# A batch pair's side work in an attention step: directly behind the transposes of exponents, in place of behind the values

## The chip, the cores and the metric

One core of a Trainium2 chip runs the kernel; the other seven are idle. The metric is the device time of one launch in microseconds (us). TensorE is called PE here, its weight loads PEld, VectorE DVE, ScalarE ACT, GpSimd POOL; SyncE (SP) only issues transfers.

## The reference

Attention with eight batches, eight heads, 576 positions and 64 channels feeds a mixture of experts. Four heads see a local window, four see every 32nd position:

```python
mask_local = (rel >= 0) & (rel < stride)                    # stride = 32
mask_strided = (rel >= 0) & (pos[None, :] % stride == pos[:, None] % stride)
scores = np.where(masks[None], scale * q @ k.transpose(0, 1, 3, 2), -1e9)
attn = np.exp(scores - scores.max(-1)); attn /= attn.sum(-1) + 1e-09
x = (attn @ v).transpose(0, 2, 1, 3).reshape(4608, 512)     # one row per token
logits = x @ w_gate + modality_bias[modality_id]            # 8 experts
e_idx = np.argmax(logits, axis=1)
for e in range(8):
    out[mask] = gate_w[mask, None] * (np.maximum(x[mask] @ w1[e], 0) @ w2[e])
```

Everything is float32. Each token goes to one expert only.

## The kernel before

**Units and steps.** The batches are taken in four pairs. A pair has eight units: local and strided ones in turn (classes `Local` and `Strided`), each for one local head of both batches or two strided heads of one batch. The main loop (L1185) runs over steps n. It is a pipeline: step n does the scores of unit n, the turn of unit n-2 and the values of unit n-3. `masks` writes the additive masks of unit n+1 into PSUM with a small bf16 product, one step ahead; `scores` adds the products of queries and keys onto them (L354 local, L449 strided), and DVE takes the maximum (L361), subtracts it (L364) and ACT exponentiates. `turn` transposes the exponents on PE (L224, tiles `t` or `ts`), and ACT or DVE copies them out. `values` multiplies them with the values (L391 and L397 local, tile `o`; L499 strided, tile `ot`).

**Order.** PE's order is that of the program (`manual_schedule`). On the other engines a scheduler sets it, save for instructions that are pinned. All products and transposes write into one pool of eight PSUM buffers (`pa`), one bank each, so an instruction that starts a tile waits until an earlier tile in its buffer has been read out.

**Pieces.** When a pair's units are done, its outputs still have to be brought into both layouts (rows of tokens, and columns for the router), routed and stored. This side work is cut into pieces, one for a step. `turn_rows` (L508) transposes one strided output block, four transposes in tile `xs`; `finish_pair` (L516) is a generator whose pieces `pop` takes one by one (L1123). With the last unit of a pair called 7, the pieces of a pair are: four transposes in step 8 and in step 9 (`xs`); eight in step 10 (`xl`, local outputs); ten in step 11 (`xl`, four buffers); the router's logits in step 12 (`lg`, L597 and L602); the transposes of the logits and four of `xs`, seven in all, in step 13; six in step 14 (`xs`, three buffers); and the ranks in step 15 (`rk`, L663 and L664). From step 13 on a row of small instructions on DVE (L623 to L680) computes each token's expert and its place. ACT copies the transposes out (L514 for `xs`, L524 for `xl`). The next pair's units run at the same time. The fourth pair has only the first two pieces inside the loop; the rest stands beside the first expert slot.

**Loads.** SP issues the loads of unit n+3 at the head of step n, the second part behind the scores of unit n. The values of unit n-1 are loaded in two parts, the second behind the products of values of this step (`after_landing`, L1217).

**Experts.** After the loop the tokens go through slots of 384 rows that share an expert: L1022 up, L1037 down, with each float32 operand split into two parts (L1058, L1059), so three products for one.

The lines that the change touches are at the end of a step:

```python
        if n + 2 < nu:
            units[n + 2].prep()
        ready = len(stores) if n >= HOLD else 9
        if n - 1 in ends or n - 2 in ends:
            turn_rows(*ends[n - 1 if n - 1 in ends else n - 2], 0 if n - 1 in ends else 1, 0)
        pop(POPS if n == nu + 2 else 1)
```

Of the kernel before, what the change touches and what calls it, by code (L numbers as in the profile page):

```python
# [41 lines left out]
POPS, POPF = 5, 3  # L42
# [6 lines left out]
EARLY, BEGIN, HOLD = 3, 27, 26  # L49
# [142 lines left out]
def attention_moe(ctx: ExitStack, tc: tile.TileContext, a, out):  # L192
# [7 lines left out]
    def pa(name):  # L200
        return ps.tile([P, 512], F32, tag="a", name=name)
# [7 lines left out]
    def keep_busy(n, name):  # L209
        t = pa(name)  # L210
        for _ in range(n):
            nc.tensor.matmul(t, idle[:, 0:P], idle[:], start=True, stop=True)  # L212
# [10 lines left out]
    def turned_to(dst, src):  # L223
        return nc.tensor.transpose(dst, src, ident)  # L224
# [14 lines left out]
    def routing_setup():  # L239

        pin(nc.sync.dma_start(rt[:], a["rt"]))
        pin(nc.sync.dma_start(ld[0:1, :], a["nul"][:, 0:2]))
        pin(nc.sync.dma_start(xd[NT:NT + 1, :].bitcast(I32), a["nul"][:, 2:2 + DM]))
        modf = lp.tile([P, 36], F32, bufs=1, name="modf")
        pin(nc.gpsimd.tensor_copy(modf[:], modi))
        nmod = lp.tile([P, 36], F32, bufs=1, name="nmod")
        pin(nc.gpsimd.tensor_scalar(nmod[:], modf[:], -1.0, 1.0, ALU.mult, ALU.add))
        bias0 = lp.tile([P, 36, E], F32, bufs=1, name="bias0")

        def bc_e(t):  # L250
            return t.unsqueeze(2).to_broadcast([P, 36, E])

        def bc_t(t):
            return t.unsqueeze(1).to_broadcast([P, 36, E])

        pin(nc.gpsimd.tensor_tensor(bias[:], bc_e(modf), bc_t(mb[:, 1, :]), ALU.mult))
        pin(nc.gpsimd.tensor_tensor(bias0[:], bc_e(nmod), bc_t(mb[:, 0, :]), ALU.mult))
        pin(nc.gpsimd.tensor_tensor(bias[:], bias[:], bias0[:], ALU.add))
# [46 lines left out]
    class Local:  # L305
# [62 lines left out]
        def turn(self):  # L368
            n, ex = self.n, self.ex
            self.et = et = ets[0]  # L370
            t1 = pa(f"t1{n}").rearrange("p (g q) -> p g q", g=4)
            for k in range(4):
                turned_to(t1[:, k, :], ex[:, 2 * k:2 * k + 2, :])
            t2 = pa(f"t2{n}")[:, :P]
            self.point = turned_to(t2, ex[:, 9:11, :])
            for par in range(2):
                r = slice(64 * par, 64 * par + 64)
                nc.scalar.copy(et[r, 0:16, par, :], t1[r].rearrange("p k (u q) -> p (k u) q", u=4))
            for jj in range(2):
                r = slice(64 * jj, 64 * jj + 64)  # L380
                nc.scalar.copy(et[r, 16:18, jj, :], t2[r, 64 * jj:64 * jj + 64].rearrange("p (b q) -> p b q", b=2))
# [127 lines left out]
    def turn_rows(bp, xt, xcs, c, k0):  # L509
        kn = min(4, 9 - k0)  # L510
        t = pa(f"xs{bp}{c}{k0}").rearrange("p (g q) -> p g q", g=4)
        for k in range(kn):
            turned_to(t[:, k, :], xcs[2 + c][:, P * (k0 + k):P * (k0 + k + 1)])
        nc.scalar.copy(xt[:, k0:k0 + kn, 256 + P * c:256 + P * c + P], t[:, :kn, :])  # L514
# [64 lines left out]
    stores, tabulating = [], []  # L579
# [281 lines left out]
    def after_landing(ins, other):  # L861
        tc.add_manual_dep(ins.ins, other.ins.name, landed, reason="transfers kept apart")
# [216 lines left out]
    units, ends = [], {}  # L1079
# [10 lines left out]
    def after(bp, xt, xcs):  # L1090
        yield from finish_pair(bp, xt, xcs)
        if bp >= EARLY:
            yield
            yield from tabulate(bp)
# [10 lines left out]
    def pop(k):  # L1105
        for _ in range(k):
            early.clear()
            while extra:
                got = next(extra[0], extra)
                if got is not extra:  # L1110
                    early.extend([got] if got else ())
                    break
                extra.pop(0)
# [43 lines left out]
    def issue(count):  # L1157
        for _ in range(count):
            if queue and (queue[0][0] >= len(plan) or plan[queue[0][0]][1] in tables):
                queue.pop(0)[1]()  # L1160
# [10 lines left out]
    nu = len(units)  # L1171
# [12 lines left out]
    for n in range(nu + 3):  # L1184
        if n + 3 < nu:  # L1185
            units[n + 3].load(0)
        if n in FILL:
            keep_busy(FILL[n], f"warm{n}")
        if n < nu:
            units[n].scores()  # L1190
        waited = bool(early)
        if n + 3 < nu:
            after_landing(units[n + 3].load(1), units[n].scored)
        if waited:
            pop(1)
        if 2 <= n <= nu + 1:
            units[n - 2].turn()
        if 1 <= n <= nu:
            ins = units[n - 1].load_values(0)
            if n >= 2:  # L1200
                after_landing(ins, units[n - 2].point)
        if n + 1 < nu:
            units[n + 1].masks()
        if n == nu + 1:
            turn(0)
        if n >= 3:
            units[n - 3].values()
        if 1 <= n <= nu:
            ins = units[n - 1].load_values(1)
            if ins and n >= 3:  # L1210
                after_landing(ins, units[n - 3].valued)
        if n >= 3:
            if n - 3 in ends:
                extra.append(after(*ends[n - 3]))
        if n == SETUP:
            routing_setup()
        if n + 2 < nu:  # L1217
            units[n + 2].prep()
        ready = len(stores) if n >= HOLD else 9
        if n - 1 in ends or n - 2 in ends:  # L1220
            turn_rows(*ends[n - 1 if n - 1 in ends else n - 2], 0 if n - 1 in ends else 1, 0)
        pop(POPS if n == nu + 2 else 1)
        for _ in range(min(ready, STORED.get(n, SPREAD[(n - 2) % 8]))):
            if stores:
                stores.pop(0)()
        if n >= BEGIN:
            issue(2)
        if n in TABLES:
            for _ in tabulating[-1]:
                break  # L1230
# [83 lines left out]
```

## Time and profile before

| What | us |
|---|---|
| Runs of the kernel | 580.5, 583.21, 588.86 |
| Median of the three | 583.21 |
| Profiled execution | 581.83 |
| Span of that execution, first to last instruction | 580.0 |
| Attention with all its side work (span's start to the first expert product) | about 151 |
| Expert slots | about 422 |

The span and the launch around it make the execution's own time: 581.83 is 1.83 us more than the span, and 1.38 us less than the median of the runs. Times in the rows below count from the span's start. A busy engine is one that has an instruction in flight; products on PE overlap, so the start of one to the start of the next tells more than its duration.

### The profile page before, as it was taken

Reading aid. Unit: us, or ns where it says so; the run is one execution under the profiler, and the core shown is the slowest. Engines: PE = TensorE matmul, PEld = TensorE weight load, DVE = VectorE, ACT = ScalarE, POOL = GpSimd, SP = SyncE. Lnnn points to the kernel's source line nnn. Section 1 sums busy time; section 2 is a strip of 40 time slices with the busy share of each in tenths; the row PEclk is TensorE's granted clock in tenths of the full one; section 3 lists DMA queues with packets and bytes.
Section 4 is the critical chain, followed back from the end, with each engine's and each line's share of the span. In section 5 each row is a group of like instructions: output and inputs, shape, how many; then the busy total and the mean of one; then the engine's idle time right before and its main releaser. Section 6 shows DMA issues by size and latency. Waiting matters only on the chain.

```text
span 580.0 us, 13584 instructions
## 1 busy us (share of the span) xinstructions
PE 564.3 (97%) x5383; PEld 495.1 (85%) x5385; DVE 381.7 (66%) x909; ACT 325.0 (56%) x646; POOL 197.2 (34%) x198
## 2 busy tenths in 40 slices
PE   9999999998999999999999999999999999999995
PEld 5878888877788899989999998989898998998884
DVE  7886977967867874676674757666475666655410
ACT  5789898897744544554454544545363555545312
POOL 3011120125464315444344334554434445320102
PEclk9999999999999999999999999999999999999999
DMA  8988898978985308566543266142414156772102
GB/s 299 332 287 298 287 326 292 327 229 296 313 296 196 118 12 308 187 199 223 154 164 74 61 211 216 47 88 73 90 33 99 52 200 174 262 162 72 56 0 76
DMA packets 62699, 104.28 MB, mean 180 GB/s; under 512 B 36451, under 2 KB 36963, under 8 KB 58532
## 3 DMA queue, kind: packets, MB, share of 16 engines
q0 software_dynamic: 15456, 57.47, 28.6%
q1 hardware_dynamic: 45636, 43.29, 25.5%
q10 hardware_dynamic: 1536, 2.58, 1.4%
q8 instruction: 44, 0.72, 0.5%
q14 instruction: 27, 0.22, 0.1%
HBM read 94.09 MB, written 19.18 MB: 195 GB/s over the span
## 4 chain that ended last, share of the span: by engine, by line
PE 82%; issue 10%; ACT 3%; DVE 2%; POOL 1%; POOLq 0%; ACTq 0%
PE h L1022 31%; PE o L1037 30%; PE s L354 3%; PE ss L449 3%; PE o L391 2%; PE ot L499 2%; PE lg L597 2%; PE xl L224 2%; PE t L224 2%; PE xs L224 1%; PE warm L212 1%; PE ts L224 1%; POOL out L1044 1%; ACT xc L507 1%; PE en L695 1%
## 5 line engine op out<-in xcount | busy, mean ns | idle before, releaser
L1059 DVE TENSOR_TENSOR wl<-raw,wh 128x512 fp32r<-128x512 f32 x176 | 115.2, 692 | 66.8 <-ACT wh L1058 56.7
L1058 ACT CAST wh<-raw 128x512 fp32r<-128x512 f32 x176 | 100.5, 619 | 99.4 <-PE o L1037 81.5
L1022 PE MATMUL h<-xh,wl 128*128 128x384 f32 x352 | 118.7, 337 | 0.0
L1022 PE MATMUL h<-xl,wh 128*128 128x384 f32 x352 | 118.2, 336 | 0.0
L1022 PE MATMUL h<-xh,wh 128*128 128x384 f32 x352 | 117.4, 337 | 0.0
L1037 PE MATMUL o<-wl,hh 128*128 128x512 f32 x264 | 104.1, 394 | 0.0
L1037 PE MATMUL o<-wh,hl 128*128 128x512 f32 x264 | 104.0, 395 | 0.0
L1037 PE MATMUL o<-wh,hh 128*128 128x512 f32 x264 | 103.2, 391 | 0.0
L1025 ACT ACTIVATE hh<-h 128x384 fp32r<-128x384 f32 x88 | 43.2, 491 | 82.4 <-PE h L1022 71.0
L1027 DVE SCALAR_TENSOR_TENSOR hl<-h,hh 128x384 fp32r<-128x384 f32 x88 | 48.9, 555 | 56.5 <-ACT hh L1025 55.1
L921 POOL DMA_INDIRECT raw<-in_w,wi x44 | 51.8, 1177 | 61.3 <-ACT hh L1025 50.8
L1022 PEld LDWEIGHTS h<-xh,wh 128*128 128x128 f32 x352 | 66.2, 188 | 4.2 <-PE xs L224 0.4
L1022 PEld LDWEIGHTS h<-xl,wh 128*128 128x128 f32 x352 | 66.1, 188 | 2.9
L1022 PEld LDWEIGHTS h<-xh,wl 128*128 128x128 f32 x352 | 66.0, 188 | 0.4 <-DVE wl L1059 0.4
L889 POOL DMA_INDIRECT fx<-xd,le x33 | 37.2, 1129 | 76.8 <-ACT wh L1058 42.2
L1037 PEld LDWEIGHTS o<-wh,hl 128*128 128x128 f32 x264 | 49.5, 188 | 10.5
L1037 PEld LDWEIGHTS o<-wl,hh 128*128 128x128 f32 x264 | 49.5, 188 | 8.6
L1037 PEld LDWEIGHTS o<-wh,hh 128*128 128x128 f32 x264 | 49.6, 188 | 8.2
L906 POOL DMA_INDIRECT le<-ld,li x33 | 35.5, 1076 | 41.9 <-DVE li L828 17.6
L1044 POOL DMA_INDIRECT out<-y,le x33 | 34.6, 1049 | 41.3 <-ACT y L1043 37.0
L589 POOL DMA_DIRECT2D xd<-xt x18 | 10.0, 558 | 64.9 <-ACT xc L507 28.2
L983 DVE COPY work<-fx 128x1536 uint16<-128x1536 uint16 x16 | 27.2, 1743 | 0.0
(215 smaller groups left out, 872.6 us busy)
## 6 DMA issues: line engine op xcount, KB each, us to landing
vv<-in_vl SPq DMA_DIRECT2D x32, 292.5 KB
qks<-in_qks SPq DMA_DIRECT2D x32, 288.0 KB
qk<-in_qkl SPq DMA_DIRECT2D x16, 304.0 KB
qk<-in_qkl SPq DMA_DIRECT2D x16, 288.0 KB
xd<-xt POOLq DMA_DIRECT2D x18, 256.0 KB
vsp<-in_vs SPq DMA_DIRECT2D x16, 256.0 KB
xd<-xt SPq DMA_DIRECT2D x9, 256.0 KB
xd<-xt ACTq DMA_DIRECT2D x2, 1024.0 KB
```

Source lines behind the costliest of these rows:

```text
L224: return nc.tensor.transpose(dst, src, ident)
L889: ins = in_turn(nc.gpsimd.indirect_dma_start(xt[:, h, :], None, xd[0:xrows, :], IOA(ap=le[:, h, 0:1], axis=0), **bounds))
L906: in_turn(nc.gpsimd.indirect_dma_start(le[:, h, :], None, ld[0:1 + last, :], IOA(ap=li[:, s, h:h + 1], axis=0)))
L921: ins = nc.gpsimd.indirect_dma_start(raws[j].rearrange("p f c -> p (f c)"), None, a["w"], IOA(ap=wi[:, s, j:j + 1], axis=0), bounds_check= ...
L983: pin(nc.vector.tensor_copy(rows[:, :, w, :], halves(xt)[:, :, :, w]))
L1022: nc.tensor.matmul(hp, w[:, a1], x[:, c, 0:size], start=(k == 0), stop=(k == 11))
L1025: steps.append(nc.scalar.activation(hh[:, 0:size], hp, AF.Relu))
L1027: nc.vector.scalar_tensor_tensor(hl[:, 0:size], hp, 0.0, hh[:, 0:size].bitcast(F32), ALU.max, ALU.subtract)
L1037: nc.tensor.matmul(os[h], hx[:, m], w[:, 512:1024], start=(f == 0 and i == 0), stop=(f == 7 and i == 2))
L1044: outs.add(in_turn(nc.gpsimd.indirect_dma_start(out, IOA(ap=le[:, i, 0:1], axis=0), y[:], None, bounds_check=NT - 1, oob_is_err=False), True))
L1058: nc.scalar.copy(wh[:, c], raw[:, c])
L1059: nc.vector.tensor_tensor(wl[:, c], raw[:, c], wh[:, c].bitcast(F32), ALU.subtract)
```

## The change

The two statements on the pieces are moved up, from the end of a step to directly behind `turn`. A piece that is popped in the step in which its pair was only just handed over (n-3 in `ends`, step 10 in the counting above) stays at the end, and so do the pops of the last two steps.

```diff
         if 2 <= n <= nu + 1:
             units[n - 2].turn()
+        ready = len(stores) if n >= HOLD else 9
+        if n - 1 in ends or n - 2 in ends:
+            turn_rows(*ends[n - 1 if n - 1 in ends else n - 2], 0 if n - 1 in ends else 1, 0)
+        beside = n <= nu + 1 and n - 3 not in ends
+        if beside:
+            pop(1)
         if 1 <= n <= nu:
             ins = units[n - 1].load_values(0)
...
-        ready = len(stores) if n >= HOLD else 9
-        if n - 1 in ends or n - 2 in ends:
-            turn_rows(*ends[n - 1 if n - 1 in ends else n - 2], 0 if n - 1 in ends else 1, 0)
-        pop(POPS if n == nu + 2 else 1)
+        if not beside:
+            pop(POPS if n == nu + 2 else 1)
```

**Place 1, step 11 of the first pair, PE.** `ts` is the turn, `s` the masks and then the scores of the next unit, `o` the values, `xl` the piece. Before:

```order
L224 MATMUL ts_1024<-cf_sb,enp_111 104x128 x4
L343 LDWEIGHTS cb_sb
L343 MATMUL s_1035<-cb_sb 128x256
L343 LDWEIGHTS cb_sb
L343 MATMUL s_1037<-cb_sb 128x320
L391 MATMUL o_1039<-vv_856,et_103 64x65 x8
L397 MATMUL o_1039<-vv_856,et_103 64x65 x2
L391 MATMUL o_1054<-vv_856,et_103 64x65 x8
L224 MATMUL xl_1070<-cf_sb,xt_123 128x128 x4
L224 MATMUL xl_1076<-cf_sb,xt_123 128x128 x4
L224 MATMUL xl_1082<-cf_sb,xt_123 128x128
L224 MATMUL xl_1085<-cf_sb,xt_123 128x128
```

Now the ten transposes of the piece stand between the turn and the masks, and the scores follow the values directly:

```order
L224 MATMUL ts_1024<-cf_sb,enp_111 104x128 x4
L224 MATMUL xl_1033<-cf_sb,xt_123 128x128 x4
L224 MATMUL xl_1039<-cf_sb,xt_123 128x128 x4
L224 MATMUL xl_1045<-cf_sb,xt_123 128x128
L224 MATMUL xl_1048<-cf_sb,xt_123 128x128
L343 LDWEIGHTS cb_sb
L343 MATMUL s_1053<-cb_sb 128x256
L343 LDWEIGHTS cb_sb
L343 MATMUL s_1055<-cb_sb 128x320
L391 MATMUL o_1057<-vv_862,et_103 64x65 x8
L397 MATMUL o_1057<-vv_862,et_103 64x65 x2
L391 MATMUL o_1072<-vv_862,et_103 64x65 x8
```

The same place on ACT, with the copies of the piece (L524) among those of the scores (L365, L366), of the turn (L488) and of the next strided unit (L464, L434). Before:

```order
L333 COPY qd_101<-qk_802 64x18x32
L365 ACTIVATE ex_902<-ex_902 128x256
L366 ACTIVATE ex_902<-ex_902 128x128
L524 COPY xc_124<-xl_966 128x512
L524 COPY xc_125<-xl_972 128x512
L488 ACTIVATE eb_1029<-ts_1024,cf_sb 104x8x36 x2
L464 ACTIVATE exs_1015<-exs_1015 128x288
L434 COPY qz_104<-qks_899 64x32x18
L524 COPY xc_124<-xl_1070 128x512
L524 COPY xc_125<-xl_1076 128x512
```

Now the first copy of step 11's piece stands directly behind the second of step 10's:

```order
L333 COPY qd_101<-qk_802 64x18x32
L524 COPY xc_124<-xl_966 128x512
L365 ACTIVATE ex_902<-ex_902 128x256
L366 ACTIVATE ex_902<-ex_902 128x128
L524 COPY xc_125<-xl_972 128x512
L524 COPY xc_124<-xl_1033 128x512
L488 ACTIVATE eb_1029<-ts_1024,cf_sb 104x8x36 x2
L524 COPY xc_125<-xl_1039 128x512
L524 COPY xc_124<-xl_1045 128x128
L524 COPY xc_125<-xl_1048 128x128
```

The piece's first copy moved up past the exponents of the strided unit (L464) and the spreading of its queries (L434).

**Place 2, step 14 of the first pair, PE.** `t` is the turn, `ss` the masks and then the scores, `ot` the values, `xs` the piece. Before:

```order
L224 MATMUL t_1332<-cf_sb,ex_1093 128x128 x4
L224 MATMUL t_1337<-cf_sb,ex_1093 128x128
L442 LDWEIGHTS cb_sb
L442 MATMUL ss_1344<-cb_sb 128x288
L499 MATMUL ot_1346<-eb_1231,vsp_114 64x72 x8
L499 MATMUL ot_1356<-eb_1231,vsp_114 64x72 x8
L224 MATMUL xs_1374<-cf_sb,xc_127 128x128 x4
L224 MATMUL xs_1380<-cf_sb,xc_126 128x128
L224 MATMUL xs_1383<-cf_sb,xc_127 128x128
L449 MATMUL ss_1344<-qks_1090,qz_105 36x18 x32
```

Now the six transposes stand in front of the masks and the values:

```order
L224 MATMUL t_1332<-cf_sb,ex_1093 128x128 x4
L224 MATMUL t_1337<-cf_sb,ex_1093 128x128
L224 MATMUL xs_1348<-cf_sb,xc_127 128x128 x4
L224 MATMUL xs_1354<-cf_sb,xc_126 128x128
L224 MATMUL xs_1357<-cf_sb,xc_127 128x128
L442 LDWEIGHTS cb_sb
L442 MATMUL ss_1361<-cb_sb 128x288
L499 MATMUL ot_1363<-eb_1231,vsp_114 64x72 x8
L499 MATMUL ot_1373<-eb_1231,vsp_114 64x72 x8
L449 MATMUL ss_1361<-qks_1090,qz_105 36x18 x32
```

The values moved back by the piece, and nothing stands between them and the scores.

## Rows read from the trace of the kernel before

**Rows 1.** The page's head: span, and PE's busy time, share and instructions.
```profile
span 580.0 us, 13584 instructions
PE 564.3 (97%) x5383; PEld 495.1 (85%) x5385; DVE 381.7 (66%) x909; ACT 325.0 (56%) x646; POOL 197.2 (34%) x198
```

**Rows 2.** Stretches: from:to, length, busy PE PEld DVE ACT POOL, PEclk, DMA share, GB/s.
```profile
0.00:151.00 151.00, 141.92 (x3235) 118.51 (x3237) 120.98 (x444) 124.50 (x284) 32.62 (x51) 1.00 0.89 300
151.00:573.00 422.00, 422.00 (x2149) 376.56 (x2148) 260.74 (x467) 199.83 (x362) 162.63 (x147) 1.00 0.45 138
```

**Rows 3.** Waits of PE, 0 to 151 us: total us, times, longest us.
```profile
PE s L354 <- issue: 2.2, 2, 1.1
...
PE o L391 <- issue: 1.2, 3, 0.4
...
PE o L391 <- ACT xt L514: 0.6, 2, 0.3
```

**Rows 4.** Waits of PEld, 0 to 160 us: the only ones put down to a load.
```profile
PEld ss L449 <- DMA qks<-in_qks: 0.8, 5, 0.2
```

**Rows 5.** Timeline of PE, two steps without a piece: start, us, what, xcount.
```profile
25.46 0.77 PE L224 MATMUL t<-cf_sb,ex 128*128 128x128 f32 x5
26.06 0.29 PE L442 MATMUL ss<-cb_sb 128*128 128x288 bf16 x1
26.28 1.22 PE L499 MATMUL ot<-eb,vsp 96*64 96x72 f32 x32
27.33 1.27 PE L449 MATMUL ss<-qks,qz 128*36 128x18 f32 x64
28.54 0.65 PE L224 MATMUL ts<-cf_sb,enp 128*104 128x128 f32 x4
...
29.87 0.29 PE L397 MATMUL o<-vv,et 128*64 128x65 f32 x4
29.99 0.64 PE L391 MATMUL o<-vv,et 128*64 128x65 f32 x16
30.46 1.22 PE L354 MATMUL s<-qk,qd 128*64 128x64 f32 x36
```

**Rows 6.** Timeline of PE, step 11 of the first pair, with ten transposes.
```profile
44.97 0.65 PE L224 MATMUL ts<-cf_sb,enp 128*104 128x128 f32 x4
...
48.24 1.27 PE L354 MATMUL s<-qk,qd 128*64 128x64 f32 x36
```

**Rows 7.** Timeline of PE, step 13 of the first pair, with seven transposes.
```profile
54.72 0.64 PE L224 MATMUL ts<-cf_sb,enp 128*96 128x128 f32 x4
...
57.65 1.27 PE L354 MATMUL s<-qk,qd 128*64 128x64 f32 x36
```

**Rows 8.** Timeline of PE, steps 14 (six transposes), 15, and 8 (four).
```profile
58.85 0.76 PE L224 MATMUL t<-cf_sb,ex 128*128 128x128 f32 x5
...
61.62 1.30 PE L449 MATMUL ss<-qks,qz 128*36 128x18 f32 x64
...
64.18 0.29 PE L397 MATMUL o<-vv,et 128*64 128x65 f32 x4
64.79 0.69 PE L391 MATMUL o<-vv,et 128*64 128x65 f32 x16 [0.32 <-ACT xt L514]
...
66.78 0.77 PE L224 MATMUL t<-cf_sb,ex 128*128 128x128 f32 x5
...
69.33 1.30 PE L449 MATMUL ss<-qks,qz 128*36 128x18 f32 x64
```

**Rows 9.** Timeline of DVE, step 14: the subtraction that frees the scores' first buffer.
```profile
60.24 0.41 DVE L364 TENSOR_TENSOR ex<-s,mx 128x256 f32<-128x256 f32 x1
```

**Rows 10.** Timeline of ACT: copies of the pieces of steps 10 and 11.
```profile
46.02 1.05 ACT L524 COPY xc<-xl 128x512 f32<-128x512 f32 x2
...
48.92 1.41 ACT L524 COPY xc<-xl 128x512 f32<-128x512 f32 x4
```

**Rows 11.** Timeline of PE: the longest run of transposes, behind the loop.
```profile
149.45 1.64 PE L224 MATMUL xl<-cf_sb,xt 128*128 128x128 f32 x13
```

## The prediction, made before the changed kernel was run

> **What bounds the kernel now.** I read the page's head first: PE is busy for 564.3 us of a span of 580.0 [rows 1], so whatever a change does to another engine counts only where PE waits for it. The windows then split the span. In the expert slots, from 151 us on, PE is busy for 422.00 of 422.00 us [rows 2]: no time is to be had there by moving work of the attention, and the change leaves PE's order in the slots alone. In the attention, the first 151 us, PE is busy for 141.92 us; the idle rest is 151.00 - 141.92 = 9.08 us, spread over some thirty steps. So the change is decided within the first 151 us, and in two quantities: what PE's instructions cost one after the other, and that idle rest.
>
> The waits of PE show what the rest is made of [rows 3]. The largest are stops with no releaser ("issue"), 2.2 us in front of local scores and 1.2 us in front of local values; nothing says that another order ends them, and I leave them. A wait that the pieces themselves cause is there too: 0.6 us, twice 0.3, in which values wait for the copy of a piece on ACT (L514). Loads hardly show: PEld waits for them 0.8 us in all, at most 0.2 [rows 4]. The share of the DMA engines in this stretch is high, 0.89 [rows 2], but PE does not wait for it.
>
> **The change, part by part.** I count a pair's units 0 to 7, as the text ahead does. A pair has seven pieces that move: steps 8, 9, 11, 12, 13, 14 and 15, with 4, 4, 10, no, 7, 6 and no transposes on the side (the logits and ranks are products). Step 10 stays. Three pairs give 21 moved pieces; the fourth pair's two have no scores behind them, and I cost them at nothing.
>
> *Saved: changes of kind on PE.* Starts, not durations, price this. A turn of five transposes takes 26.06 - 25.46 = 0.60 us, 0.12 for each [rows 5]. From turn to scores a step without a piece takes 27.33 - 25.46 = 1.87 us if the turn is local, 30.46 - 28.54 = 1.92 us if it is strided [rows 5]. The same stretch with a piece between values and scores:
> - four transposes: 69.33 - 66.78 = 2.55, so 0.68 more than 1.87; four cost 0.48 by rate, 0.20 is extra [rows 8];
> - six: 61.62 - 58.85 = 2.77, 0.90 more against 0.72: 0.18 [rows 8];
> - seven: 57.65 - 54.72 = 2.93, 1.01 more against 0.84: 0.17 [rows 7];
> - ten: 48.24 - 44.97 = 3.27, 1.35 more against 1.20: 0.15 [rows 6].
>
> The extra hardly depends on the number, so it is a price of going from products to transposes and back. Behind `turn` the piece follows transposes, and its last one is followed by the masks as the turn's last one was: the extra should go. For a pair that is 0.20 + 0.20 + 0.15 + 0.17 + 0.18 = 0.90 us (steps 8, 9, 11, 13, 14), for three pairs 2.7 us. The pieces of step 12 and 15 are products of their own kind; no row shows them between transposes and masks. They can save an extra of 0.20 or add one; I take 0.1 saved, as they too break up a row of values and scores now, six times 0.1 = 0.6 us, with both ends kept (+1.2 and -1.2). Sum: 3.3 us saved.
>
> *Saved: the wait for L514.* In step 15 the second group of values starts 64.79 - 64.18 = 0.61 us after the first group's last part [rows 8], where a step without the wait needs 29.99 - 29.87 = 0.12 [rows 5]. Its buffer was held by the piece of step 14. The change turns the buffers round, and there the values get one that ACT reads out earlier. Two such waits are in the trace [rows 3], 2 x 0.49 = 1.0 us saved. The other bound is 0: a wait of the same size stays.
>
> *Added: buffers asked for earlier.* All these tiles share eight buffers. Each moved piece takes one to four of them before masks and values, which so take later ones, still in use.
> - Step 14. The values' first group gets a buffer of scores, freed by the first subtraction on DVE, at 60.24 + 0.41 = 60.65 us [rows 9]. With the piece ahead of it, it would start at 58.85 + 0.60 (turn) + 0.72 (piece) + 0.22 (masks, 26.28 - 26.06) = 60.39 us [rows 5, 8]. It waits 0.26 us; three pairs, 0.8 us.
> - Step 11, the piece with four buffers. The second mask would start at 44.97 + 0.48 + 1.20 + 0.11 = 46.76 us, but two copies of step 10's piece on ACT hold the buffers until 46.02 + 1.05 = 47.07 [rows 6, 10]: 0.31 us. Then the values need the buffer of this piece's own first copy, which is half of a copy pair (0.5 us) behind 47.07, at some 47.57, where they would be ready at 47.30: 0.27 us more. Three pairs: 0.58 x 3 = 1.7 us.
>
> If ACT does the copies in a worse order, the waits double, 5.0 us: the four copies of this piece take 1.41 us now [rows 10], and their place among exponents is what changes. The least is none, if ACT comes sooner than in before.
>
> *Moved at no cost.* The values start later in their step by the piece's length, 0.5 to 1.2 us; what reads them is a step away, and the scores, which start DVE's and ACT's chain for the next turn, come no later, since the piece was ahead of them before too. SP's order is the same as before; its one transfer tied to the values (the second part of the next ones) is issued later by the piece's length, and what stands behind it on SP waits for the next scores anyway. The cover is a lead of about a step (some 3 us) in the loads; gone, it would show as PE waiting for `vv` or `vsp`, where now it waits at most 0.2 us on any load [rows 4]. POOL's stores keep their order but for one exchange of neighbours; it is busy for 32.62 of 151 us [rows 2]. The small routing instructions on DVE get their input a little sooner; DVE is busy for 120.98 of 151 us [rows 2], so they find gaps, and where they push a maximum or a subtraction of scores back, that is in the doubled waits.
>
> *Sum.* -3.3 - 1.0 + 0.8 + 1.7 = -1.8 us. Against the profiled execution's own time that is 581.83 - 1.8 = 580.0 us. This execution is 1.38 us below the median of the runs, 583.21; the four times that are known (580.5, 581.83, 583.21, 588.86) have the middle 582.5, and 582.5 - 1.8 gives my number, **580.7 us**. The best bound is 2.7 + 1.2 + 1.0 = -4.9, the worst -2.7 + 1.2 + 5.0 = +3.5 us.
>
> **A rule against the change.** In the transposes that the trace has in a row, thirteen behind the loop, PE starts one about every 0.12 us, and the granted clock is 1.00, the level of 2.4 GHz, throughout the 151 us [rows 2, 11]. The Trainium skill (TensorE: Matmul & The Clock Gate, Part 4: PE-mode transpose) says that the clock gate does not engage its full rate for transposes, which do not count as PE-busy in the same way. Here the row of thirteen did not lower it, so the trace so far speaks against that rule; it becomes rival C.
>
> **Rivals.**
> - *A, all is given back (0.14).* The extra goes, but masks and values wait for as much: 582.5 to 583.2 us. For it: every engine is near its limit in some steps (ACT 124.50 of 151 us busy [rows 2]). Against: most of a pair's pieces take two buffers or less.
> - *B, a buffer wait in every step with a piece (0.06).* The place is the first mask or value behind the piece. If each of the 21 waits 0.49 us, the size of the wait in step 15 [rows 8], that is 10.3 - 3.3 = +7.0: 589.5 us. It makes the kernel slower once the wait is above 3.3 / 21 = 0.16 us per piece, and by over 2% from (11.65 + 3.3) / 21 = 0.71. For it: the piece now stands between the freeing of buffers and the masks, which are wanted soonest. Against: in steps 8, 9, 12, 13 and 15 I find no late buffer.
> - *C, the clock falls (0.02).* Step 11 now has 4 + 10 = 14 transposes in a row, one more than the longest row of before [rows 11]. If the clock then went to its lower level of 1.2 GHz until the step's end, masks, values and scores (31.68 - 28.54 - 0.48 = 2.66 us, with 30.46 + 1.22 = 31.68 [rows 5]) would take twice as long: three times +2.66 = +8.0, 588.7 us.
> - *D, the stops go too (0.02).* Most of the 9.08 us of idle time [rows 2] vanish with the 3.3: 12 us, some 570.5. Nothing shows why they should.
> - The forecast has 0.76. That the change does not do what it says is out: the order that is shown ahead has the pieces where the words put them.
>
> **Range and chances.** Two per cent of 583.21 are 11.65 us, about what a measurement of this kernel can tell from no change: below 571.6 is faster, above 594.9 slower. Low end: the fastest run with the best bound, 580.5 - 4.9 = 575.6 us. High end: 582.5 + 3.5 = 586.0, and up to 588.86 - 1.8 = 587.0, since one of the runs lay that high. That leaves out D and most of B and C. Faster 0.03 (D and a little), slower 0.04 (the upper tail of B, and C if it lasts for longer than a step), the same 0.93.
>
> **What would show it.** The extra: 2.55 - 0.20 = 2.35 us from turn to scores in the steps with four transposes, and likewise 2.59 for six, 2.76 for seven, 3.12 for ten, before new waits. The freed wait: no line "values wait for ACT, L514". The new waits: values of step 14 waiting for DVE's L364, masks and values of step 11 waiting for ACT's L524, none above 0.4 us. Expert slots: 422 us again. I am wrong in the cause if the turn-to-scores times don't shrink, wrong in the size if lines of PE waiting for L524, L365 or L488 add up to over 5 us, and rival C shows as a granted clock under 1.00 in step 11.

## The result, and the profile after

The changed kernel is slower: 586.18 us (median of 20 runs, 582.02 to 589.06) against 582.2 us (20 runs, 579.41 to 588.86), a ratio of 1.0061 with an interval of 1.0042 to 1.0079, some 3.6 us. I had forecast 1.8 us less. The profiled execution took 587.72 us, 5.9 us more than that of before; its granted clock is lower than in most of the runs, so it shows the cause large.

The page's head and two stretches of the changed kernel (columns as in rows 1 and 2; the first product of the experts now starts at 157.31 us, before at 151.05):

```profile
span 585.9 us, 13587 instructions
PE 564.6 (96%) x5383; PEld 498.2 (85%) x5385; DVE 381.5 (65%) x909; ACT 324.6 (55%) x646; POOL 194.9 (33%) x198
...
0.00:157.00 157.00, 142.29 (x3235) 121.59 (x3237) 120.69 (x439) 123.79 (x283) 30.89 (x51) 0.97 0.85 281
157.00:579.00 422.00, 421.69 (x2147) 376.36 (x2147) 260.81 (x471) 200.08 (x363) 162.07 (x146) 1.00 0.45 141
```

Against [rows 1, 2]: the expert slots take the same 422 us, and PE's busy time in the attention is nearly the same, 142.29 us against 141.92 (what the change saves and what a lower clock costs, both priced below, pull it in opposite ways). The idle time is not, 14.7 us against 9.08, and the granted clock has fallen from 1.00 to 0.97. The waits of PE, 0 to 157 us (columns as in rows 3):

```profile
PE o L391 <- issue: 4.9, 3, 2.1
...
PE ct L756 <- ACT fx L887: 1.2, 1, 1.2
PE ss L449 <- issue: 1.0, 2, 0.5
PE ts L224 <- issue: 1.0, 2, 0.6
PE ot L499 <- DVE ex L364: 0.8, 2, 0.4
```

The wait for L514 of [rows 3] is gone, as forecast. The stops without a releaser are not: in the rows of PE's timeline up to 140 us they come to 7.9 us where before had 4.25, and two are longer than any before. The first of these two, in PE's timeline:

```profile
70.86 0.56 PE L391 MATMUL o<-vv,et 128*64 128x65 f32 x11
73.54 0.59 PE L391 MATMUL o<-vv,et 128*64 128x65 f32 x5 [2.12 <-issue]
...
74.90 2.15 PE L354 MATMUL s<-qk,qd 128*64 128x64 f32 x36
```

In the middle of a group of values, with its operands there, PE stops for 2.12 us. What follows is slow as well: the 36 products of scores last 2.15 us, where [rows 5] have 1.22. Stretches of half a microsecond (columns as in rows 2) show why:

```profile
71.00:71.50 0.50, 0.42 (x11) 0.28 (x9) 0.50 (x2) 0.48 (x2) 0.48 (x2) 1.00 1.13 444
72.50:73.00 0.50, 0.00 (x0) 0.00 (x0) 0.00 (x0) 0.50 (x2) 0.50 (x2) 1.00 0.99 379
73.00:73.50 0.50, 0.00 (x0) 0.00 (x0) 0.00 (x0) 0.50 (x2) 0.34 (x2) 0.92 1.03 401
74.00:74.50 0.50, 0.50 (x16) 0.50 (x14) 0.12 (x1) 0.22 (x1) 0.00 (x0) 0.50 1.05 421
76.50:77.00 0.50, 0.50 (x15) 0.50 (x13) 0.50 (x4) 0.00 (x0) 0.00 (x0) 0.67 0.69 191
77.00:77.50 0.50, 0.50 (x13) 0.50 (x11) 0.50 (x2) 0.00 (x0) 0.27 (x1) 1.00 0.87 337
```

The clock stays at 1.00 until 0.1 us before PE goes on, falls to 0.50, the level of 1.2 GHz, and stays there for 3.4 us. By estimate half the work is done in them: 1.7 us lost on top of the stop. The same happens at 104.2 us, behind a stop of 2.02 us, and at 141.7 us, behind two stops of 0.53 and 0.48 and 0.3 us of work between. By that estimate the three falls cost 5.1 us.

**What the stops are.** The count of PE and PEld instructions from the start to each stop tells (columns as in rows 2, PE's and PEld's counts in the brackets):

```profile
0.00:24.00 24.00, 22.56 (x470) 16.33 (x473) 19.24 (x51) 15.61 (x34) 4.64 (x10) 1.00 0.92 314
0.00:28.80 28.80, 26.90 (x595) 20.21 (x598) 23.37 (x64) 19.72 (x43) 4.64 (x10) 1.00 0.93 318
0.00:38.80 38.80, 36.32 (x845) 28.68 (x848) 32.17 (x89) 29.06 (x64) 7.30 (x16) 1.00 0.91 310
...
0.00:71.50 71.50, 67.06 (x1598) 55.35 (x1600) 58.49 (x186) 57.98 (x130) 11.39 (x24) 1.00 0.89 299
0.00:101.50 101.50, 94.30 (x2226) 79.25 (x2228) 79.11 (x259) 81.44 (x185) 16.46 (x32) 0.98 0.88 294
```

The sums are 943, 1193, 1693, 3198 and 4454: steps of 250, 500 (2 x 250), 1505 (6 x 251) and 1256 (5 x 251). PE stops at the ends of blocks of about 250 instructions. The page's list of queues has one named "instruction" that moves blocks of 0.72 MB / 44 = 16 KB:

```profile
q8 instruction: 44, 0.72, 0.5%
```

Two windows of the queues (packets, MB, share of the 16 DMA engines), one from the end of the block before to just ahead of the stop, one of 0.25 us at the stop:

```profile
q1 hardware_dynamic: 655, 1.44, 85.7%
q0 software_dynamic: 82, 0.27, 14.0%
q14 instruction: 1, 0.01, 0.4%
```

```profile
q0 software_dynamic: 19, 0.07, 64.3%
q1 hardware_dynamic: 16, 0.04, 39.6%
q8 instruction: 1, 0.02, 23.5%
```

From 66.5 to 71.25 us the loads (q1) and the stores of rows (q0) hold the DMA engines to 99.7%, and no packet of q8 starts. It starts at 71.3 us, PE has run through its instructions at 71.4, and goes on 2.2 us after the packet's start. Each of these stops is code that came late, and the same sign is in the other traces: of the twenty kernels measured here, those below included, 63 stops up to 140 us have no releaser and last longer than 0.53 us, and every one stands at the end of a block and ends 2.2 to 2.7 us behind the start of a packet of q8. None of them is in the three kernels without loads. The Trainium skill (Runtime: NRT & Kernel Launch, Instruction fetch mechanics) says that code is fetched in 16 KiB blocks of 256 instructions over a DMA queue of the sequencer's own, and that the cost of a block's end is mostly hidden. The trace agrees with the block, 250 recorded instructions and 16 KB; that it is hidden does not hold here.

Not every shorter stop is of this kind. Of the 7.9 us, 6.6 stand at such block ends (in before 3.1 of 4.25). The two ahead of the third fall do not: they stand at the same products of scores, in step 14 of the third pair, when the stream is shifted by 56, 118 or 180 places, and in the changed kernel without loads, where the granted clock stays at 1.00. The two in the changed kernel, and then in that without loads (L462 is L449):

```profile
139.62 0.30 PE L449 MATMUL ss<-qks,qz 128*36 128x18 f32 x4 [0.53 <-issue]
140.39 1.00 PE L449 MATMUL ss<-qks,qz 128*36 128x18 f32 x46 [0.48 <-issue]
```

```profile
131.58 0.23 PE L462 MATMUL ss<-qks,qz 128*36 128x18 f32 x2 [0.48 <-issue]
132.31 1.02 PE L462 MATMUL ss<-qks,qz 128*36 128x18 f32 x47 [0.50 <-issue]
```

What makes them is open, so of the three falls only two follow late code.

### The profile page after: what moved, and what is told of

Same layout as the page of the kernel before. It is cut to its first block, busy times and chain, and to the rows that moved or that the text cites. A ratio compares the mean times of both kernels' runs of the same rounds, so it can differ in the third digit from the quotient of the medians.

```text
span 585.9 us, 13587 instructions
## 1 busy us (share of the span) xinstructions
PE 564.6 (96%) x5383; PEld 498.2 (85%) x5385; DVE 381.5 (65%) x909; ACT 324.6 (55%) x646; POOL 194.9 (33%) x198
## 4 chain that ended last, share of the span: by engine, by line
PE 81%; issue 11%; DVE 2%; ACT 2%; POOL 1%; DMA 0%; POOLq 0%; ACTq 0%
PE h L1022 31%; PE o L1037 29%; PE o L391 3%; PE s L354 3%; PE ss L449 3%; PE ot L499 3%; PE t L224 2%; PE lg L597 1%; PE ts L224 1%; PE warm L212 1%; PE xs L224 1%; POOL out L1044 1%; ACT xc L524 1%; PE xt L224 1%; PE en L695 1%
## 5 line engine op out<-in xcount | busy, mean ns | idle before, releaser
L921 POOL DMA_INDIRECT raw<-in_w,wi x44 | 50.6, 1150 | 63.7 <-ACT hh L1025 50.0
L889 POOL DMA_INDIRECT fx<-xd,le x33 | 35.6, 1078 | 78.1 <-ACT wh L1058 25.1
L391 PEld LDWEIGHTS o<-vv,et 128*64 128x64 f32 x512 | 19.8, 148 | 10.6 <-issue 6.7
```

The lines of the kernel that those rows point to most:

```text
L391: self.valued = nc.tensor.matmul(o[64 * jj:64 * jj + 64, k, :], et[:, u, :, :].rearrange("p g q -> p (g q)"), vv[:, u, :], start=True, sto ...
L889: ins = in_turn(nc.gpsimd.indirect_dma_start(xt[:, h, :], None, xd[0:xrows, :], IOA(ap=le[:, h, 0:1], axis=0), **bounds))
L921: ins = nc.gpsimd.indirect_dma_start(raws[j].rearrange("p f c -> p (f c)"), None, a["w"], IOA(ap=wi[:, s, j:j + 1], axis=0), bounds_check= ...
```

## The experiments

Three theories, as the expectations name them. **Theory 1**: late code behind full DMA engines is the loss. **Theory 2**: the same, but only by chance, because the change moved the ends of the blocks to bad places. **Theory 3**: the buffer waits that I had priced (masks and values waiting for copies on ACT and DVE) are larger than I took them. Ratios are to the kernel before on the same chip (its median there was 578.8 to 582.1 us).

**Without loads.** In each kernel the loads of units beyond the first two of a kind are left out; values and strided loads likewise:

```diff
         def load(self, part):
             n = self.n
+            if n >= 2:
+                self.qk = held["qk", n % 2]
+                return None
```

> The kernel before, with the loads of every unit beyond the first two of each kind left out (those units reuse the operands that are there, so the output is another, and the routing may fill the slots another way). Theory 1 (late code): PE's stops without a releaser come because the instructions that PE needs next are fetched late while the loads fill the DMA engines; without loads, no stop in the loop above 0.3 us, against 1.13 and 1.11 us in the trace of before, and the attention ends 3 to 5 us sooner than at 151 us. Theory 3 (buffers: masks and values that wait for copies on ACT and DVE make the change slow): the stops have nothing to do with it, the attention ends within 2 us of 151.

> The changed kernel with the same loads left out. Theory 1: no stop above 0.3 us, a granted clock of 1.00 through the whole loop (0.50 for 3.4 us at three places in the trace of after), and 2 to 5 us less than the kernel before without these loads: the gain on PE that the loads hide. Theory 2 (it is only chance where the ends of fetched blocks fall in the changed order): the same here. Theory 3: 3 to 6 us more than the kernel before without these loads, with PE waiting for ACT's L524 and DVE's L364 as with the loads.

> That kernel (steps 11 and 14 in their old place) with the loads beyond the first two units of each kind left out, as in the two kernels run so before (other output, other filling of slots). From the steps of those two traces (steps 8, 9, 12, 13 and 15 together 1.6 us shorter in the changed one) three pairs should take 3.5 to 5.5 us less than in the kernel before without loads, from the first pair's first piece to the third pair's last, with no wait for L524 and L364 in the values. With loads the same edit gained 0.7 us: the rest would be what the loads take back. If the three pairs gain under 2 us here too, the loads are not what hides it.

The routing fills more slots with these operands (638.44, 639.96 and 636.25 us, the medians of four, four and one runs, the last on another chip), so I compare stretches of the loop, of one profile each. From the turn of step 8 of the first pair to the end of the third pair's step 15:

| | before | changed | steps 11 and 14 in the old place |
|---|---|---|---|
| without loads, us | 103.76 | 103.69 | 100.80 |
| stops without a releaser up to 140 us, longest | 0.46 | 0.50 | 0.51 |

The long stops are gone (what is left lies a little above the 0.3 us that I had set), and the granted clock is 1.00 in every stretch up to 145 us, in both orders: theory 1 or 2. The attention ended at 147.54 us in the order before, 3.5 us sooner, as theory 1 had it, and at 147.14 us in the changed one. But the gain of the change itself is 0.07 us, where theory 1 said 2 to 5 and theory 3 a loss of 3 to 6, and the part without steps 11 and 14 gains 3.0, a little under its 3.5 to 5.5. These are single profiles. By the medians of whole runs the changed order is 1.5 us slower even without loads, and the runs of the two overlap (637.65 to 639.37 and 638.55 to 641.43 us), so that without loads the change is worth something between nothing and a loss of 1.5 us. Step 11 of the first pair, PE's timeline without loads, in the kernel before and then in the changed one (L351 here is L343, L362 is L354, L537 is L524):

```profile
43.47 0.65 PE L224 MATMUL ts<-cf_sb,enp 128*104 128x128 f32 x4
43.95 0.41 PE L351 MATMUL s<-cb_sb 128*128 128x256 bf16 x2
...
46.73 1.27 PE L362 MATMUL s<-qk,qd 128*64 128x64 f32 x36
```

```profile
42.85 0.65 PE L224 MATMUL ts<-cf_sb,enp 128*104 128x128 f32 x4
43.33 1.25 PE L224 MATMUL xl<-cf_sb,xt 128*128 128x128 f32 x10
44.42 0.27 PE L351 MATMUL s<-cb_sb 128*128 128x256 bf16 x1
45.43 0.30 PE L351 MATMUL s<-cb_sb 128*128 128x320 bf16 x1 [0.73 <-ACT xc L537]
...
47.02 1.22 PE L362 MATMUL s<-qk,qd 128*64 128x64 f32 x36
```

From turn to scores 4.17 us against 3.26: the second mask waits 0.73 us for a copy of a piece. So theory 3 has its part, in full view only here. The waits of PE of this kernel up to 140 us (L372 is L364):

```profile
PE s L351 <- ACT xc L537: 2.7, 5, 1.0
...
PE ot L512 <- DVE ex L372: 1.3, 3, 0.5
...
PE o L399 <- ACT xc L537: 0.6, 3, 0.2
```

The queues, 60 to 75 us of the changed kernel without loads, for comparison with 99.7% above:

```profile
q0 software_dynamic: 347, 1.16, 20.5%
q8 instruction: 3, 0.05, 1.2%
```

Located in narrow windows, a packet of q8 starts 0.7 us on average behind the end of the block before (21 blocks each, at most 1.9 and 3.0 us), against 1.9 us (at most 3.8) in before and 2.0 us (at most 5.0) in after with their loads.

**PE's stream shifted.** Tiny products in place of wide warm-up products in steps 2 and 3 put everything behind further back in the stream:

```diff
-FILL = {2: 4, 3: 6}
+FILL = {2: 2, 3: 3}
...
+            for _ in range(32):
+                nc.tensor.matmul(t[0:16, 0:16], idle[:, 0:16], idle[:, 0:16], start=True, stop=True)
```

> The kernel before with 64 tiny products in place of 5 of the 10 wide warm-up products in steps 2 and 3: about the same work on PE (64 x 0.02 us against 5 x 0.24 us), but every later instruction stands 118 places further back in PE's stream, so the ends of fetched blocks (some 250 instructions apart) fall elsewhere. Theory 1: within 2 us of before (580 to 584). Theory 2: it moves as the change moved it, by 2 to 6 us in either direction. Theory 3: unchanged.

> The changed kernel with the same 118 places of shift. Theory 1: slower than the shifted kernel before by 2 to 6 us, again with stops at block ends and at least one fall of the clock. Theory 2: its time comes to that of before or lower (578 to 583), with the stops at other places and shorter. Theory 3: 586 as without the shift, with the same waits for L524 and L364.

> The kernel before, PE's stream shifted by 56 places (32 tiny products in place of 4 wide warm-up products). Theory 1 (late code by nature): 0 to 3 us above before. Theory 2 (where block ends fall): anything from -3 to +6 us, as the shift by 118 places gave +5 to +6.

> The changed kernel with the same shift of 56 places. Theory 1: 2 to 5 us above the kernel before with that shift. Theory 2: the difference of the two can have either sign, -4 to +4 us.

> The kernel before, shifted by 180 places (100 tiny products in place of all 10 wide ones of steps 2 and 3; some 0.5 us more work). Theory 1: 0 to 3 us above before. Theory 2: -3 to +6 us.

> The changed kernel with the same shift of 180 places. Theory 1: 2 to 5 us above the kernel before with that shift. Theory 2: -4 to +4 us.

| shift, places | before, us | changed, us | difference | stops up to 140 us: before, changed |
|---|---|---|---|---|
| 0 | 582.2 | 586.18 | +4.0 | 4.25, 7.9 |
| 56 | 583.44 | 588.85 | +5.4 | 1.7, 10.2 |
| 118 | 587.25 | 589.99 | +2.7 | 4.0, 11.6 |
| 180 | 583.98 | 589.51 | +5.5 | 3.8, 7.8 |

The two kernels of a row ran on one chip; the rows are of different chips. The intervals of 56 (1.0004 to 1.0039 against 1.0067 to 1.0154) and of 180 (1.0003 to 1.0044 against 1.0068 to 1.0163) lie apart. Those of 118 (1.0046 to 1.0189 against 1.0056 to 1.0202, four runs each) do not: the ratios are 1.0118 and 1.0129, and the +2.7 of the medians shows nothing. So with two other places of the block ends the changed order is slower again, and with a third it gains nothing: theory 2 alone does not explain the loss. But where the blocks end counts for as much as the change: a shift alone moves the kernel before by 1 to 6 us. The largest groups of stops with a shift of 56, among PE's waits up to 140 us, of the order before and then of the changed one (L392 is L391, L355 is L354, L450 is L449):

```profile
PE o L392 <- issue: 1.2, 1, 1.2
```

```profile
PE o L392 <- issue: 4.5, 2, 3.1
PE s L355 <- issue: 2.6, 2, 2.2
PE ss L450 <- issue: 2.3, 1, 2.3
```

**The change in two halves.** Steps 11 and 14 in the old place, and only these two moved:

```diff
-        beside = n <= nu + 1 and n - 3 not in ends
+        beside = n <= nu + 1 and n - 3 not in ends and n % 8 not in (3, 6)
```

> The changed kernel, with the pieces of steps 11 and 14 (ten and six transposes, the ones behind which PE waits for ACT's L524 and DVE's L364) back in their old place; the other pieces stay moved. In the traces without loads these waits make up 3.3 and 1.3 us; what the two pieces save on PE is 0.33 us for each of three pairs. Theory 3 (the buffer waits are the loss): 586.2 - 4.6 + 1.0 = 582.6 us or a little less, level with the kernel before or faster. Theory 1 (late code under full DMA engines is the loss; PE that is ready sooner only meets it sooner): 584 to 587 us, with stops of 1 to 2 us at block ends still there.

> The other half: only the pieces of steps 11 and 14 moved, all else as before. Theory 3: the whole loss, 582.2 + 4.6 - 1.0 = 585.8 us, with PE waiting for L524 and L364. Theory 1: 581 to 584 us, because PE is hardly ahead of before anywhere.

Steps 11 and 14 in the old place: ratio 0.9988 (0.9966 to 1.0010), 578.22 us against 578.9, and stops of 4.3 us, none above 0.84. Only these two moved: 1.0036 (1.0014 to 1.0058), 2.1 us more; its profile, the slowest of its twelve runs (585.2 us), has stops of 5.1 us. The first is what theory 3 said and not theory 1, the second in between. The halves' differences, -0.7 and +2.1, do not add up to +3.6 either: the rest appears only with both.

**More work for PE.** The masks are written a second time, by the same product, ahead of 20 steps' scores, in the place that the pieces had:

```diff
         if n < nu:
+            if n in TWICE:
+                units[n].masks_again()
             units[n].scores()
```

> The changed kernel with the masks written a second time ahead of the scores of the 20 steps that follow a moved piece: no other wait and no other buffer, but 0.22 us (strided) or 0.34 us (local) more work on PE each time, some 5.6 us in all. Theory 1: the time rises by less than half of that, to 584 to 588 us, since a slower PE meets the late code less; the stops get shorter. Theory 3: 586.2 + 5.6 = 591.8 us.

Ratio 1.0090 (1.0058 to 1.0123), against 1.0061 of the changed kernel: 5.6 us of work cost some 1.7 us, and the stops fall from 7.9 to 2.7 us. That is theory 1's number and not theory 3's. The run does not part the two as cleanly as I had meant, though: the waits for L524 and L364 fall as well, from 1.9 to 0.6 us (one profile each).

**The loads paced in other ways.** One transfer for two; the values' first part behind the masks; the values' second part behind the masks:

```diff
-            c = slice(0, 18 * 32) if part == 0 else slice(18 * 32, 37 * 32)
+            if part:
+                return None
+            c = slice(0, 37 * 32)
```

> The changed kernel with queries and keys of a unit loaded by one transfer at the head of the step in place of two (rows of 4.6 or 4.7 KB a partition in place of 2.3), the second of which waited for the scores. Theory 1: if longer rows take the DMA engines less time, code comes sooner and the time falls to 580 to 584 us; if the transfers only bunch up more, 587 to 592 us with longer stops. Theory 3: 586 us, as the order on PE, ACT and DVE is the same.

Ratio 1.0123 (1.0094 to 1.0153), 586.74 us on a chip where before took 578.9: theory 1's second case, with stops of 2.94 and 2.30 us and 11 us of them up to 140 us. That the transfers bunch up more was not measured.

```diff
-                after_landing(ins, units[n - 2].point)
+                after_landing(ins, units[n + 1].masked if n + 1 < nu else units[n - 2].point)
```

> The changed kernel; the first part of a step's values is loaded behind the masks, not behind the turn, so that in a step with a moved piece this transfer starts later by the length of the piece (0.5 to 1.2 us). Order on PE, ACT and DVE unchanged. In the traces the changed kernel has the two loads of queries and keys issued within 1.0 to 1.2 us in the steps with a moved piece (before: 2.2 to 3.2), and the third load right behind. Theory 1 in its present form (the change bunches the transfers, and fetched code comes late behind the bunch): 2 to 4 us less than the changed kernel, a ratio to before of 0.997 to 1.003. Theory 3 (buffer waits alone): the ratio stays at 1.006.

> The same gate in the kernel with the pieces of steps 11 and 14 in their old place (0.9988 of before without the gate). Theory 1: another 1 to 4 us less, ratio 0.992 to 0.998: faster than both. Theory 3: 0.9988 again.

1.0056 (1.0029 to 1.0083) and 1.0003 (0.9976 to 1.0029): no change beyond the intervals. Starting the third load later wins nothing back.

```diff
-                after_landing(ins, units[n - 3].valued)
+                after_landing(ins, units[n + 1].masked if n + 1 < nu else units[n - 2].point)
```

> The changed kernel; the second part of a step's values is loaded behind the masks (some 1.2 us before the values' end), not behind the values, so that one transfer and not two starts there. Theory 1 with the bunch as its cause: ratio to before 0.997 to 1.003. Without: 1.004 to 1.010, as the changed kernel itself (1.006).

> The same in the kernel before. Theory 1 with the bunch as its cause: 0.994 to 0.999. Without: 0.999 to 1.003.

> The same in the kernel with the pieces of steps 11 and 14 in their old place (0.9988 without it). Theory 1 with the bunch as its cause: 0.993 to 0.997, faster than both. Without: 0.997 to 1.002.

1.0060 (1.0031 to 1.0089), 0.9996 (0.9959 to 1.0032) and 0.9958 (0.9930 to 0.9985). The changed kernel gains nothing, so the bunch of two loads behind the values is not what makes it slow. The third kernel, with the five other pieces moved and the values' second part loaded sooner, takes 577.94 us against 578.84 by the medians and is the one version faster than both; as one of several tried, by 0.4%, it is a hint more than a result.

## Why the prediction was wrong

The forecast was -1.8 us with most of its chance, and a range up to 587.0 that holds the 586.18; the sign is wrong. Two steps failed, one of them a step of two lines.

**The saving was right.** Turn to scores with four transposes is 68.40 - 66.09 = 2.31 us in the changed kernel where I had said 2.35, with six 2.90 where 2.59 and a wait of 0.26 were forecast:

```profile
58.82 0.77 PE L224 MATMUL t<-cf_sb,ex 128*128 128x128 f32 x5
...
61.72 1.30 PE L449 MATMUL ss<-qks,qz 128*36 128x18 f32 x64
...
66.09 0.77 PE L224 MATMUL t<-cf_sb,ex 128*128 128x128 f32 x5
...
68.40 1.27 PE L449 MATMUL ss<-qks,qz 128*36 128x18 f32 x64
```

Compared with [rows 8], the price of going from products to transposes and back is gone. Without loads the five pieces other than steps 11 and 14 gain 103.76 - 100.80 = 3.0 us; my terms for them were (0.20 + 0.20 + 0.17) x 3 + 0.6 + 1.0 = 3.3. That the two sums agree is partly luck: they come from single profiles on two chips, and 2.7 of the 3.0 us fall in the third pair, where step 12 of the order before takes 6.67 us and not the 5.28 of the first two pairs. In the first two pairs steps 8, 9, 13 and 15 do gain some 1.1 us a pair from turn to turn, as forecast, but steps 10 and 11 give 0.8 and 1.3 us back although their pieces were not moved.

**The new buffer waits were mis-sized.** I had the place right, step 11's masks behind L524 and step 14's values behind L364, but not the size: without loads these waits come to 2.7 + 0.6 us for the copies and 1.3 us for the subtraction, 4.6 us where I had 1.7 + 0.8 = 2.5. The kernel with steps 11 and 14 in the old place is 103.69 - 100.80 = 2.9 us shorter, where my terms made 0.8 + 1.7 - 3 x (0.15 + 0.18) = 1.5; but again nearly all of it is in the third pair, with the two odd stops of its step 14, and the first two pairs differ by 0.05 us in sum. Step 11 took 0.85, 1.59 and 0.70 us longer in the three pairs where I had 0.43. With its piece in the old place it still took 0.37, 1.26 and 0.34 us longer, so the move of this piece alone cost 0.33 to 0.48 us, what I had said; the rest seems to come with the other moved pieces, for which I had found no late buffer. I had taken L524's end from the trace of before [rows 10]; in the changed kernel these copies stand among others. With this the change is worth -0.07 us by the profiles without loads, my rival A, and in size it comes within the 5.0 us that I had kept as the worst.

**The step that failed**: "The largest are stops with no releaser ('issue') ...; nothing says that another order ends them, and I leave them." Nothing said either that another order lengthens them, and it does: 1.7 to 4.25 us in five profiles of the order before (with its shifts and the last gate), 6.9 to 11.6 us in six of the changed one. With the falls of the clock behind the longest I put the remaining 3.6 us down to this: it is the difference between -0.07 us without loads and +3.6 with them (2.1 us, if the medians without loads are taken). I had read a DMA share of 0.89 [rows 2] and no wait of PE for a load [rows 4] as "loads are hidden"; they were, but PE's own code comes through the same engines. I had named a lead of about a step as the cover of the loads; for the code I had asked for no cover. It is about one block: the packet that ended the stop at 71.42 us had started about 5 us behind the end of the block before, and that was too late.

**The rivals.** C had the fall of the clock, at the level it has, and a price of 8.0 us (5.1 in the profiled execution), but for another reason: not a row of 14 transposes, for in step 11 the granted clock stays at 1.00, but a stop of 2 us (and once the two odd stops of 0.5 us). B's place, a wait in every step, did not come; D neither.

**What stays open** is why this order brings its code later. It is not only where blocks end, and not the two bunches of loads that I took apart. What is shown is that the long stops need the loads, that the loss needs steps 11 and 14 moved as well as the others, and that 5.6 us more work between values and scores, where the pieces stood, takes 5.2 us of the stops away in the one profile. Whether that is the place or merely a slower PE I did not separate.

## What to carry to other kernels

A stop of PE in the middle of a group, without a releaser, is worth counting instructions for. Here the long ones stood some 250 instructions or a multiple apart and ended a fixed time behind a packet of the instruction queue: they were fetches of code, late while the loads held the DMA engines, and an order of the same instructions that loads the same bytes made them longer. At the DMA share of 0.89 of this attention a gain on PE was not to be booked in full; trying the edit once without its loads tells how much is taken back, if it is run often enough to beat the scatter. Split an edit that moves many pieces: with two of the seven pieces put back, the loss was gone.

## What the hardware showed that I had not expected

- Going from transposes to products of float32 and back costs PE 0.15 to 0.20 us a piece of four to ten transposes [rows 6 to 8]; behind other transposes this price is gone (2.55 to 2.31 us with four).
- A block of code is asked for up to about 5 us behind the end of the block before when the loads fill the DMA engines (99.7% in the window above), and PE goes on 2.2 to 2.7 us after the packet's start: a stop of up to 3.06 us at a block's end (the shift of 56), against 0.51 us at most without loads.
- In the profiled execution the granted clock falls to 0.50 three times, for 3.4 us each: 0.1 us before the end of a stop of 2.12 us, 0.6 us behind one of 2.02 us, and 1.3 us behind the two of 0.53 and 0.48 us. A stop of this length does not always bring a fall: those of 2.18 us (the shift of 118, order before), 2.08 us (the same shift, changed order) and 2.21 us (the shift of 56, changed order) were followed by none, nor were those of 1.13 and 1.11 us in before.
